# The first steps of a chunked-attention and SoLU-FFN kernel listed anew

## The chip, the cores and the metric

The kernel runs on one core of a Trainium2 chip. The metric is the device time of one execution in microseconds (us). Three runs of the kernel before gave a median of 476.33 us, from 475.26 to 476.84.

## The reference, cut to what matters

Attention in chunks of 64 tokens for 8 batches and 8 heads, then one feed-forward layer on all 4608 tokens. The weights arrive as 8-byte floats, q, k, v as 4-byte ones.

```
q, k, v: (8, 8, 576, 64); chunks of 64
scores = (q_c @ k_c.T) / 8; scores -= max; attn = exp(scores)
attn /= sum(attn) + 1e-9; x = (attn @ v_c) as (4608, 512)
h = x @ w_in                       # (4608, 1024)
sm = softmax(h); solu = h * sm
ln = (solu - mean) / sqrt(var + 1e-6) * g_ln
out = ln @ w_out                   # (4608, 512)
```

## The kernel before

The 4608 tokens are 36 tiles of 128. A tile i goes through transposes of q and k (N), scores (S), a softmax in two parts (A, B), a transpose of the attention (T), values (V), the first product with w_in (M), the SoLU in two parts (X, Y), its variance (R), the turn of z (Z or z) and the second product with w_out in three thirds (F). Products with weights are exact to more bits than one pass gives: each weight and each operand is a high and a low part, and three products are added (24 matmuls of 128x512). Tiles 0 and 1 (`FM = 2`) use the weights whole, in 16 passes, straight from the buffer `w_a`.

The weights are 8 units of 1 MB raw: 0 to 3 are w_in (128 rows each), 4 to 7 are w_out. A unit m is loaded (P), clamped and scaled (c: a clamp on VectorE or GpSimd, then an activation on ScalarE), put together from its two words (C: a shift and a 16-bit addition on VectorE), rounded to its high part (t, ScalarE), and its low part is found for each half (D, the difference, on VectorE or GpSimd). Tile 0's product takes unit m as soon as C:m is done (it is begun in four pieces, one per unit, the four words `M:0`); tile 2's product, the first with three products, needs t and D of units 0 to 3.

Everything before tile 5's product is a list of such steps in one string, `START`. A word is a step; where a step has several parts (a generator), each further mention of the same word runs its next part: `N:1:0` first puts the transposes on TensorE, the second time the copy out of PSUM. `keep_in_program_order` holds every engine's instructions in the order of the list, so each engine takes its own in turn and waits at the first whose data is missing. SyncE (SP) issues nearly all loads, in the list's order too: n is q and k of a tile as they lie in memory (256 KB each), v the values (three loads for a tile below 6 that doesn't straddle two batches), P a unit, q:8 eight of the 32 loads of batch 2's q and k in turned form. W:x is a filler: two matmuls of the identity whose result nobody reads. Two PSUM banks `po` are shared by N, T, z, G and F; during `START` the scores have one bank (`sx`) and the values one (`sy`), and the first products one pair (`ph`), so S:i+1 waits for A:i, V:i+1 for the read of V:i, and M:i+1 for the last read of M:i's result by Y:i (VectorE).

From tile 5 on a loop runs at a fixed order. Its first TensorE steps are M:5, S:8, V:6, S:9, V:7 and then the second product of tile 2. V:6 and V:7 read an attention that U:6 and U:7 turned on VectorE and that SP and GpSimd then move by DMA (`attn_t<-a_b`), and tile 2's operand comes by the DMAs of Z:3 (`z_t<-z_b`).

The tuples ahead of the pools say which engine does a part: `NV_DVE` copies of N on VectorE (else ScalarE), `CL_DVE` clamps on VectorE (else GpSimd), `TV_DVE` copies of T, `NORM_POOL` normalisations (B) on GpSimd (else VectorE), `SUB_POOL` the low parts (D) on GpSimd, `MEAN_POOL` the shift by the mean (Y's second part) on GpSimd (else ScalarE).

Of the kernel before, what the change touches and what calls it, by code (L numbers as in the profile page):

```python
# [12 lines left out]
AF = mybir.ActivationFunctionType  # L13
# [3 lines left out]


START = """
W:41 W:42 n:0 n:1 N:0:1 N:0:0 N:0:0 N:0:1 N:1:0 n:2 S:0 N:2:1 N:1:0 A:0 A:0 P0 P1 P:2 N:1:1 B:0  # L20
P:1 c:0 c:2 N:1:1 W:43 c:0 N:2:0 S:1 W:44 W:45 W:46 N:2:1 N:2:0 n:3 c:2 C:0 A:1 A:1 C:0 B:0 c:1
B:1 S:2 T:0 N:3:0 T:0 W:47 g W:4 c:1 N:3:0 A:2 v:0 C:2 N:3:1 P:3 G P:4 t:0 V:0 N:3:1 n:4 C:1 B:1
G V:0 A:2 S:3 C:1 C:2 T:1 B:2 B:2 c:3 c:3 M:0 t:2 M:0 A:3 C:3 T:1 M:0 v:1 A:3 C:3 c:4 B:3 M:0
N:4:1 X:0 t:1 N:4:0 c:4 n:5 N:4:1 T:2 v:2 B:3 N:4:0 n:6 X:0 V:1 C:4 v:3 P:5 P:6 D:1:0 T:2 Y:0
S:4 T:3 C:4 N:5:0 V:1 A:4 t:3 A:4 P:7 T:3 D:1:1 M:1 t:4 N:5:1 D:3:1 B:4 D:2:1 N:5:0 D:0:1 D:2:0
D:0:0 Y:0 N:5:1 V:2 N:6:1 D:3:0 v:4 D:4:0 N:6:0 c:5 B:4 D:4:1 V:2 S:5 X:1 n:7 N:6:1 X:1 V:2 Y:1
z:0:1 N:6:0 V:3 z:0:1 c:5 R:0 A:5 z:0:0 C:5 A:5 z:0:0 V:3 C:5 M:2 z:0:1 T:4 c:6 B:5 z:0:0 V:3
Q:2 S:6 t:5 c:6 N:7:0 T:4 X:2 C:6 V:4 q:8 v:5 N:7:0 B:5 n:8 D:5:1 c:7 D:5:0 T:5 X:2 Y:2 C:6 T:5
F c:7 Y:2 t:6 C:7 N:7:1 C:7 N:7:1 D:6:1 D:6:0 M:3 F t:7 D:7:0 A:6 V:4 N:8:0 V:4 D:7:1 R:2 q:8
Y:1 N:8:0 V:5 S:7 X:3 Z:2 X:3 N:8:1 Y:3 A:7 N:8:1 A:6 q:8 q:8 F z:1:0 z:1:0 R:1 A:7 B:6 v:6  # L30
z:1:0 M:4 V:5 B:7 B:6 Y:3 U:6 o:0 B:7 Z:3 z:1:1 U:7 z:1:1 v:7 X:4 o:0 X:4 F z:1:1 Y:4 R:3 F K:9
F o:1 Y:4 o:1 V:5 R:4
"""


# [23 lines left out]
def chunk_attention_then_solu_ffn(  # L59
# [35 lines left out]
    MS = nc.gpsimd
    ORD = 5
# [28 lines left out]
    g_sb = const.tile([P, NFC], F32, name="g_sb")  # L125
    g_row = const.tile([NFC, P], F32, name="g_row")
# [10 lines left out]
    HALF = FF // 2  # L137
    raw_words = 2 if w_in.dtype != F32 else 1
# [28 lines left out]
    def unit_scale(x):  # L167
# [71 lines left out]
    QT, KT, V, QS, KS = {}, {}, {}, {}, {}  # L239
# [98 lines left out]
    def turn_natural(i, x):  # L338
# [25 lines left out]
    def attn(i, part):  # L364
        return (sx, sy)[i % 2 if order.on else part][:, :, part]
# [46 lines left out]
    def softmax_b(i):  # L412
# [15 lines left out]
    def attn_transpose(i):  # L428
# [148 lines left out]
    def solu_b(i):  # L577
# [162 lines left out]
    def load_first():  # L740
        load_pair(0)
        sync.dma_start(*early[0])
# [57 lines left out]
    def product():  # L800
# [150 lines left out]
```

## Time and profile before

| | |
|---|---|
| median of 3 runs | 476.33 us |
| the profiled execution | 477.21 us |
| its span | 475.3 us |
| TensorE busy, share of the span | 97% |
| VectorE, ScalarE, GpSimd | 78%, 53%, 34% |

The profile is of one execution: the time outside its span is 1.91 us. Engines are PE (TensorE), PEld (its weight loads), DVE (VectorE), ACT (ScalarE), POOL (GpSimd), SP (SyncE); SPq is the issue of a DMA on SP. A busy TensorE can be one at half its clock; the granted clock stands in the windows as PEclk, 1.00 being full.

### The profile page before, as it was taken

The numbers are of one execution on the slowest core, as the hardware profiler recorded it, in microseconds if no ns is written. First come the engines' busy times: TensorE is split into PE (matmuls) and PEld (weight loads), VectorE is DVE, ScalarE is ACT, GpSimd is POOL, SyncE is SP. The second block draws the span as 40 slices with busy tenths as digits, with TensorE's granted clock in tenths as the row PEclk, the third lists the DMA queues.
The fourth block names the chain that finished last, engine by engine and source line by source line (L and its number), as shares of the span: only waits on it lengthen the run. The fifth ranks groups of instructions, "written<-read, shape, count | busy, mean of one in ns | idle before, by whom it ended". The sixth has DMA issues, their size and how long they took to land.

```text
span 475.3 us, 10986 instructions
## 1 busy us (share of the span) xinstructions
PE 461.9 (97%) x4193; PEld 378.3 (80%) x4193; DVE 368.8 (78%) x511; ACT 249.9 (53%) x402; POOL 160.2 (34%) x305
## 2 busy tenths in 40 slices
PE   6699999999999999999999999999999999999996
PEld 5555888888888888888888888888888888888886
DVE  2799988798888787878788878797979797945430
ACT  2565985546464645454545555555555555554551
POOL 0338556350505050505050505032515141413300
PEclk9799999999999999999999999999999999999999
DMA  9999877878787877697348596948644435333211
GB/s 225 302 248 325 135 134 154 197 181 161 173 164 174 157 179 143 154 168 172 84 125 167 140 188 147 181 123 182 152 111 110 113 85 140 97 103 103 75 44 46
DMA packets 192996, 72.05 MB, mean 152 GB/s; under 512 B 177128, under 2 KB 177648, under 8 KB 192560
## 3 DMA queue, kind: packets, MB, share of 16 engines
q1 hardware_dynamic: 186528, 58.63, 55.4%
q0 software_dynamic: 6272, 12.60, 10.1%
q8 instruction: 33, 0.54, 0.5%
q14 instruction: 19, 0.16, 0.1%
q10 hardware_dynamic: 144, 0.13, 0.1%
HBM read 36.70 MB, written 9.44 MB: 97 GB/s over the span
## 4 chain that ended last, share of the span: by engine, by line
PE 94%; DMA 2%; SPq 2%; DVE 1%; issue 0%; DVEq 0%
PE po L50 44%; PE ph L50 42%; PE sx L50 5%; PE sy L50 4%; DMA nat_z<-in_q_dram 2%; SPq L50 2%; DVE w_a L50 0%; DVE z L50 0%; DVE h_nmax L50 0%; DVE qT L50 0%; DVE o_sb L50 0%; DVEq L50 0%
## 5 line engine op out<-in xcount | busy, mean ns | idle before, releaser
L50 PE MATMUL po<-wo_l,z_h 128*128 128x512 f32 x280 | 110.8, 396 | 0.0
L50 ACT ACTIVATE z<-ph,h_nmax 128x1024 f32<-128x1024 f32 x36 | 40.2, 1117 | 131.6 <-DVE h_nmax L50 131.5
L50 PE MATMUL po<-wo_h,z_h 128*128 128x512 f32 x280 | 109.3, 390 | 0.0
L50 PE MATMUL po<-wo_h,z_l 128*128 128x512 f32 x280 | 109.2, 390 | 0.0
L50 PE MATMUL ph<-wi_l,x_h 128*128 128x512 f32 x272 | 106.1, 390 | 0.0
L50 PE MATMUL ph<-wi_h,x_h 128*128 128x512 f32 x272 | 105.8, 389 | 0.0
L50 POOL TENSOR_TENSOR u<-ssq,eps 128x1 f32<-128x1 f32 x36 | 6.8, 189 | 225.6 <-ACT sq L50 225.6
L50 POOL DMA_DIRECT2D z_t<-z_b x136 | 67.7, 505 | 16.6 <-DVE z_b L50 10.5
L50 PE MATMUL ph<-wi_h,x_l 128*128 128x512 f32 x272 | 72.7, 389 | 0.0
L50 DVE TENSOR_REDUCE h_nmax<-ph 128x1 f32<-128x1024 f32 x36 | 44.0, 1221 | 34.8 <-PE ph L50 34.8
L50 PEld LDWEIGHTS po<-wo_l,z_h 128*128 128x128 f32 x280 | 52.5, 188 | 11.4
L50 PEld LDWEIGHTS po<-wo_h,z_l 128*128 128x128 f32 x280 | 52.6, 188 | 11.0
L50 PEld LDWEIGHTS po<-wo_h,z_h 128*128 128x128 f32 x280 | 52.6, 188 | 10.4
L50 PEld LDWEIGHTS ph<-wi_l,x_h 128*128 128x128 f32 x272 | 51.1, 188 | 10.7 <-issue 0.2
L50 PEld LDWEIGHTS ph<-wi_h,x_l 128*128 128x128 f32 x272 | 51.0, 188 | 10.6
L50 PEld LDWEIGHTS ph<-wi_h,x_h 128*128 128x128 f32 x272 | 51.1, 188 | 10.5
L50 DVE TENSOR_TENSOR z_l<-z_t,z_h 128x1024 fp32r<-128x1024 f32 (+1 forms) x35 | 40.7, 1164 | 21.0 <-ACT z_h L50 21.0
L50 DVE SCALAR_TENSOR_TENSOR z<-ph,z 128x1024 f32<-128x1024 f32 x36 | 44.0, 1224 | 13.8 <-ACT z L50 13.7
L50 ACT ACTIVATE z<-z,z_sum 128x1024 f32<-128x1024 f32 x34 | 39.2, 1153 | 21.4 <-DVE z L50 20.3
L50 DVE STREAM_TRANSPOSE z_b<-z 128x1024 f32<-128x1024 f32 x33 | 39.9, 1209 | 6.6 <-ACT z L50 3.1
L50 ACT ACTIVATE o_sb<-po,r 128x512 f32<-128x512 f32 (+1 forms) x36 | 24.3, 675 | 28.5 <-POOL r L50 20.8
L50 ACT ACTIVATE sq<-z 128x1024 bf16<-128x1024 f32 x36 | 37.6, 1043 | 2.5 <-POOL z L50 2.5
(88 smaller groups left out, 621.8 us busy)
## 6 DMA issues: line engine op xcount, KB each, us to landing
out_dram<-o_sb SPq DMA_DIRECT2D x35, 256.0 KB, 2.5
z_t<-z_b SPq DMA_DIRECT2D x128, 64.0 KB, 2.9
z_t<-z_b POOLq DMA_DIRECT2D x128, 64.0 KB, 2.8
q_st<-in_q_dram SPq DMA_DIRECT2D x96, 72.0 KB, 3.2
k_st<-in_k_dram SPq DMA_DIRECT2D x96, 72.0 KB, 2.9
v_sb<-in_v_dram SPq DMA_DIRECT2D x27, 256.0 KB, 4.3
w_raw<-in_moe_w_out_dram SPq DMA_DIRECT2D x4, 1024.0 KB, 7.2
attn_t<-a_b POOLq DMA_DIRECT2D x60, 64.0 KB, 3.6
```

Of the source, the lines that this page charges most:

```text
L50: ins = make(*args, **kwargs)
```

## The change

The list `START` is replaced by another with the same steps: the eight fillers, every transpose, product and load occur in both. v of tile 0 is loaded third (after q and k of tile 0), units 0 and 1 ahead of q and k of tile 2, unit 2 behind them as two loads of half its columns, unit 3 right behind that and ahead of tile 3. The parts are dealt to the engines anew. g goes by ScalarE's DMA queue. Units 4 and 5 (`GM_ACT`) are multiplied by g on ScalarE in place and then copied to the high part by a second ScalarE instruction, so that the low part is a plain difference.

```diff
 START = """
-W:41 W:42 n:0 n:1 N:0:1 N:0:0 N:0:0 N:0:1 N:1:0 n:2 S:0 N:2:1 N:1:0 A:0 A:0 P0 P1 P:2 N:1:1 B:0
-P:1 c:0 c:2 N:1:1 W:43 c:0 N:2:0 S:1 W:44 W:45 W:46 N:2:1 N:2:0 n:3 c:2 C:0 A:1 A:1 C:0 B:0 c:1
-B:1 S:2 T:0 N:3:0 T:0 W:47 g W:4 c:1 N:3:0 A:2 v:0 C:2 N:3:1 P:3 G P:4 t:0 V:0 N:3:1 n:4 C:1 B:1
-G V:0 A:2 S:3 C:1 C:2 T:1 B:2 B:2 c:3 c:3 M:0 t:2 M:0 A:3 C:3 T:1 M:0 v:1 A:3 C:3 c:4 B:3 M:0
-N:4:1 X:0 t:1 N:4:0 c:4 n:5 N:4:1 T:2 v:2 B:3 N:4:0 n:6 X:0 V:1 C:4 v:3 P:5 P:6 D:1:0 T:2 Y:0
-S:4 T:3 C:4 N:5:0 V:1 A:4 t:3 A:4 P:7 T:3 D:1:1 M:1 t:4 N:5:1 D:3:1 B:4 D:2:1 N:5:0 D:0:1 D:2:0
...
+n:0 W:41 W:45 W:43 N:0:1 v:0 N:0:0 n:1 W:42 P0 P1 c:0 P:1 N:0:1 n:2 N:0:0 P:2 W:44 S:0 N:1:0
+A:0 N:1:0 A:0 N:1:1 W:4 N:1:1 P:3 B:0 c:0 B:0 S:1 A:1 A:1 T:0 T:0 n:3 N:2:0 c:1 v:1 v:3
+c:1 N:2:1 N:2:1 n:4 W:47 N:2:0 W:46 v:2 C:0 C:0 V:0 c:2 C:1 C:1 n:5 S:2 P:5 V:0 B:1 B:1
+T:1 g A:2 c:2 P:4 t:1 C:2 c:3 c:3 T:1 C:2 M:0 M:0 N:3:0 t:2 M:0 C:3 A:2 N:3:1 C:3
+t:3 P:6 M:0 B:2 B:2 D:3:1 D:3:0 N:3:0 N:3:1 T:2 X:0 D:1:0 V:1 V:1 S:3 D:2:0 T:2 N:4:1 X:0 N:4:0
+V:2 A:3 N:4:1 N:4:0 t:0 S:4 Y:0 P:7 n:6 V:2 Y:0 R:0 A:4 M:1 D:1:1 D:0:0 A:3 B:3 A:4 V:2
+v:4 c:5 B:4 N:5:1 B:4 B:3 D:2:1 c:4 T:3 N:5:1 T:3 N:5:0 X:1 T:4 X:1 n:7 D:0:1 v:6 V:3 T:4
+N:5:0 S:5 Y:1 G A:5 c:4 C:4 z:0:1 c:5 c:6 G M:2 c:6 z:0:1 C:4 C:6 z:0:1 V:3 C:6 t:4
+D:4:1 X:2 N:6:1 N:6:1 z:0:0 N:6:0 n:8 D:4:0 c:7 V:3 X:2 N:6:0 V:4 Y:2 t:6 D:6:1 C:5 A:5 C:5 S:6
+B:5 B:5 Y:2 V:4 Z:2 z:0:0 z:0:0 N:7:0 v:5 t:5 D:6:0 D:5:1 D:5:0 N:7:0 R:2 M:3 X:3 T:5 F F
+T:5 X:3 V:4 Y:3 Y:1 c:7 C:7 N:7:1 N:7:1 Q:2 A:6 C:7 M:4 t:7 D:7:0 A:6 z:1:0 z:1:0 Y:3 D:7:1
+q:8 B:6 B:6 z:1:0 F q:8 X:4 S:7 A:7 q:8 R:1 v:7 V:5 o:0 z:1:1 z:1:1 U:6 q:8 z:1:1 F
+N:8:0 F Z:3 A:7 N:8:0 N:8:1 X:4 B:7 Y:4 R:3 N:8:1 B:7 V:5 Y:4 V:5 R:4 U:7 o:0 K:9 F
+o:1 o:1
...
-    NV_DVE = ((0, 1), (1, 0), (2, 1), (4, 0), (6, 1), (9, 1),)
-    MEAN_POOL = (3, 4,)
-    CL_DVE = (0, 3, 4,)
-    TV_DVE = (3,)
-    SUB_POOL = ((0, 0), (0, 1), (1, 0), (1, 1), (2, 0), (2, 1), (3, 0), (3, 1), (7, 0), (7, 1),)
-    NORM_POOL = (0, 1, 2, 3, 4, 5, 6, 7,)
+    NV_DVE = ((0, 1), (1, 1), (5, 0), (6, 0), (7, 1), (8, 1), (9, 1))
+    MEAN_POOL = (1, 3)
+    CL_DVE = (1, 3)
+    TV_DVE = ()
+    GM_ACT = (4, 5)
+    SUB_POOL = ((0, 1), (1, 0), (1, 1), (2, 0), (3, 0), (4, 0), (4, 1), (5, 1), (6, 1))
+    NORM_POOL = (0, 4, 5, 6)
...
-    XV_DVE = ()
+    HALF_IN = (2,)
+    XV_DVE = (1, 2)
...
                 g = g_sb[:, 2 * m + y:2 * m + y + 1]
-                act.activation(top[:, y], a[:, y], AF.Copy, scale=g)
+                act.activation(
+                    a[:, y] if x in GM_ACT else top[:, y], a[:, y], AF.Copy, scale=g
+                )
+            if x in GM_ACT:
+                act.copy(top, a)
...
-        sync.dma_start(g_row, g_ln.rearrange("(a p) -> a p", p=P))
+        nc.scalar.dma_start(g_row, g_ln.rearrange("(a p) -> a p", p=P))
```

## Rows read from the trace of the kernel before

**Rows 1.** The page: busy times, then the chain that ended last
```profile
PE 461.9 (97%) x4193; PEld 378.3 (80%) x4193; DVE 368.8 (78%) x511; ACT 249.9 (53%) x402; POOL 160.2 (34%) x305
...
PE 94%; DMA 2%; SPq 2%; DVE 1%; issue 0%; DVEq 0%
```

**Rows 2.** Waits of TensorE from 0 to 40 us: total, times, longest
```profile
PE sx L50 <- DVE e L50: 2.9, 1, 2.9
...
PE po L50 <- DMA nat_z<-in_q_dram: 1.1, 1, 1.1
PE ph L50 <- DVE z L50: 0.9, 1, 0.9
```

**Rows 3.** Timeline of TensorE: start, length, what, idle before it
```profile
18.27 0.66 PE L50 MATMUL po<-ident,e 128*128 128x128 f32 x4
20.04 1.09 PE L50 MATMUL po<-ident,nat_z 128*128 128x128 f32 x4 [1.12 <-DMA nat_z<-in_q_dram]
...
26.23 7.15 PE L50 MATMUL ph<-w_a,x_f 128*128 128x512 f32 x16
...
38.27 7.10 PE L50 MATMUL ph<-w_a,x_f 128*128 128x512 f32 x16 [0.95 <-DVE z L50]
```

**Rows 4.** Windows: stretch, length, busy by engine, PEclk, DMA share, GB/s
```profile
6.00:7.00 1.00, 1.00 (x6) 0.87 (x5) 0.55 (x1) 0.00 (x0) 0.00 (x0) 1.00 1.40 218
11.00:12.00 1.00, 0.68 (x7) 0.49 (x6) 0.62 (x1) 0.83 (x2) 0.00 (x0) 1.00 1.08 434
23.00:24.00 1.00, 1.00 (x12) 0.65 (x13) 0.07 (x1) 0.22 (x1) 0.00 (x0) 0.50 1.04 418
...
45.00:60.00 15.00, 15.00 (x225) 12.12 (x224) 14.53 (x20) 12.88 (x23) 9.37 (x9) 1.00 0.85 181
```

**Rows 5.** Timeline of SP's DMA issues
```profile
9.71 5.12 SPq L50 DMA_DIRECT2D nat_z<-in_k_dram  x1
14.87 2.76 SPq L50 DMA_DIRECT2D g_row<-in_moe_g_ln_dram  x1
...
20.08 0.60 SPq L50 DMA_DIRECT2D w_raw<-in_moe_w_in_dram  x1
...
60.70 6.90 SPq L50 DMA_DIRECT2D q_st<-in_q_dram  x8
67.72 9.83 SPq L50 DMA_DIRECT2D k_st<-in_k_dram  x16
...
78.71 5.39 SPq L50 DMA_DIRECT2D z_t<-z_b  x8
84.27 2.42 SPq L50 DMA_DIRECT2D attn_t<-a_b  x4
```

**Rows 6.** Timeline: the first clamps of units 0 and 1
```profile
13.59 0.69 DVE L50 TENSOR_SCALAR w_a<-w_raw 128x1024 f32<-128x1024 f32 x1 [1.27 <-DMA w_raw<-in_moe_w_in_dram]
...
18.88 1.42 POOL L50 TENSOR_SCALAR w_a<-w_raw 128x1024 f32<-128x1024 f32 x1 [0.71 <-DMA w_raw<-in_moe_w_in_dram]
```

**Rows 7.** Groups of the tile w_a, 13 to 66 us: shortest/median/longest ns
```profile
L50 ACT ACTIVATE w_a<-w_a x8: 1057/1057/1079, 14.3 to 59.3; 128x1024 f32<-128x1024 f32 x8
L50 DVE TENSOR_SCALAR w_a<-w_a x8: 667/684/1830, 15.4 to 61.4; 128x1024 uint32<-128x1024 uint32 x8
L50 DVE SCALAR_TENSOR_TENSOR w_a<-w_raw,w_a x8: 1326/1382/2248, 17.4 to 62.1; 128x1024 uint16<-128x1024 uint32 x8
L50 POOL TENSOR_TENSOR wi_l<-w_a,wi_h x8: 1265/1277/2301, 33.9 to 45.5; 128x512 fp32r<-128x512 f32 x8
...
L50 DVE SCALAR_TENSOR_TENSOR wo_l<-w_a,g_sb,wo_h x6: 726/736/1758, 43.3 to 64.1; 128x512 fp32r<-128x512 f32 x6
```

**Rows 8.** DMA issues at 86.4 us: KB each, us from issue to landing
```profile
attn_t<-a_b SPq DMA_DIRECT2D x1, 64.0 KB, 2.2
```

**Rows 9.** Timeline of TensorE where the attention moved by DMA is first read
```profile
89.69 0.75 PE L50 MATMUL sx<-attn_t,v_sb 64*64 64x64 f32 x29
```

**Rows 10.** The chain that ended last, in order of time, at M:2
```profile
49.88 5.67 PE ph L50 x24
```

More of the change, by code (lines that the diff above doesn't have):

```diff
@@ L19 @@
 START = """
-W:41 W:42 n:0 n:1 N:0:1 N:0:0 N:0:0 N:0:1 N:1:0 n:2 S:0 N:2:1 N:1:0 A:0 A:0 P0 P1 P:2 N:1:1 B:0
-P:1 c:0 c:2 N:1:1 W:43 c:0 N:2:0 S:1 W:44 W:45 W:46 N:2:1 N:2:0 n:3 c:2 C:0 A:1 A:1 C:0 B:0 c:1
-B:1 S:2 T:0 N:3:0 T:0 W:47 g W:4 c:1 N:3:0 A:2 v:0 C:2 N:3:1 P:3 G P:4 t:0 V:0 N:3:1 n:4 C:1 B:1
-G V:0 A:2 S:3 C:1 C:2 T:1 B:2 B:2 c:3 c:3 M:0 t:2 M:0 A:3 C:3 T:1 M:0 v:1 A:3 C:3 c:4 B:3 M:0
-N:4:1 X:0 t:1 N:4:0 c:4 n:5 N:4:1 T:2 v:2 B:3 N:4:0 n:6 X:0 V:1 C:4 v:3 P:5 P:6 D:1:0 T:2 Y:0
-S:4 T:3 C:4 N:5:0 V:1 A:4 t:3 A:4 P:7 T:3 D:1:1 M:1 t:4 N:5:1 D:3:1 B:4 D:2:1 N:5:0 D:0:1 D:2:0
[L26 to L32, printed above, removed]
+n:0 W:41 W:45 W:43 N:0:1 v:0 N:0:0 n:1 W:42 P0 P1 c:0 P:1 N:0:1 n:2 N:0:0 P:2 W:44 S:0 N:1:0
[12 more added lines that the diff above has]
+o:1 o:1
 """
@@ L161, in load_pair @@
         else:
-            sync.dma_start(dst, src)
+            cut = HALF * raw_words if x in HALF_IN else 2 * HALF * raw_words
+            if x >= NCC:
+                sync.dma_start(dst, src)
+            else:
+                for n in range(0, 2 * HALF * raw_words, cut):
+                    sync.dma_start(dst[:, n:n + cut], src[:, n:n + cut])
         raws[x] = raw
@@ L221, in unit_rest @@
             low = wo_l[:, 2 * m + y, :]
-            g = g_sb[:, 2 * m + y:2 * m + y + 1]
+            if x not in GM_ACT:
+                g = g_sb[:, 2 * m + y:2 * m + y + 1]
         of, part = a[:, y], top[:, y].bitcast(F32)
```

## The prediction

> **What bounds the kernel now.** I read busy times and the chain first [rows 1]: TensorE is busy for 97% of the span and makes 94% of the chain that ended last, so an edit counts only if TensorE begins its work earlier or is stopped later. Then where it stands still: its waits are all ahead of 40 us [rows 2], the last one 0.9 us in front of tile 1's product, which starts at 38.27 [rows 3]. From there it has one instruction behind the other to the end. Third, its clock [rows 4]: PEclk is 0.50 in the window at 23 us (full would be 2.4 GHz, this is 1.2), after the engine had done nothing from 18.93 (18.27 + 0.66) to 20.04 and, before that, for the 2.9 us of the longest wait; a set of four transposes then takes 1.09 us [rows 3]. By 26.23 it is back: tile 0's 16 passes take 7.15 us, tile 1's 7.10. Fourth, why it waits: for scores behind VectorE (2.9 us), and for q of tile 3 (1.1) [rows 2]. Loads all go through SP, which is held at 9.71 for 5.12 us by k of tile 3 and then for 2.76 us by the tiny g, so that unit 3 is issued only at 20.08 [rows 5].
>
> The steps are the same before and after, the eight fillers too. So two questions: how much earlier, for the same work done, TensorE has its unbroken run, and whether the new deal among the engines breaks that run later.
>
> **The loads.** q, k and v move at 218 GB/s, weights at 434 [rows 4]: 256 KB (0.262 MB) take 1.2 us, a unit (1.05 MB) 2.4 us. v of tile 0 now lies ahead of the units (+1.2), q and k of tile 2 behind units 0 and 1 (-2.4). Unit 0 was there at 13.59 [rows 6]: now 13.59 - 2.4 + 1.2 = 12.4. The third unit in the queue was there at 18.88 [rows 6]; the second now at 18.88 - 2.4 - 2.4 + 1.2 = 15.3, the third (unit 2, with tile 2 ahead again) at 20.1, unit 3 right behind at 22.5. Tile 2's q, by tile 3's of before (20.04, three units and three tiles ahead of it [rows 3]), comes at 20.04 - 2.4 - 2.4 + 1.2 = 16.4, its k at 17.6; tile 3's at 20.04 + 2.4 + 1.2 = 23.6 and 24.8. Unit 2's two halves cost SP one more issue (0.6 at most [rows 5]) and gain nothing, as its clamp reads both. g leaves SP: that frees 2.76 us, which only the loads behind tile 3 see; on ScalarE it costs between nothing and the same 2.76 us. I take 0.5, hidden, as no step of TensorE waits for ScalarE there by less than that.
>
> **Up to tile 0's product.** Unit 0's clamp is now on GpSimd (1.1, at most 1.42 [rows 6]) and tile 0's normalisation behind it, another 1.1: T:0 at 14.6 in place of 18.27. TensorE then waits for tile 2 until 16.4, so its clock will fall as before. From 16.4 it has N:2, two fillers, V:0, S:2, T:1; before, from 20.04 to 26.23, it had the same kinds of steps and G, at the low clock for most of it: 6.2 us [rows 3]. So M:0 begins at 22.6, 3.6 earlier. But N:3's two sets, done before M:0 in the old order, now stand between its pieces (1.2 us): it ends at 22.6 + 7.15 + 1.2 = 31.0, in place of 33.4. Are the units there? Unit 2: 20.1, clamp 1.1, ScalarE 1.06, shift 0.7, addition 1.35 [rows 7], with some 2 us behind other steps: 26.3, wanted at 26.8. Unit 3: 22.5, the same chain with its clamp behind unit 2's shift on VectorE: 28.2, wanted at 29.2. Both just make it.
>
> **Tile 1's product.** After M:0 VectorE takes the maximum, ScalarE the exponential and VectorE the product before `ph` is free: 38.27 - 33.4 = 4.9 us before [rows 3]. The new list puts tile 1's x and tile 3's softmax between them on VectorE, where a copy and unit 4's shift stood. That shift was one of the slow ones (up to 1.83 us where 0.68 is usual [rows 7]). I keep 4.9: M:1 at 35.9, 2.4 earlier. Less work lies ahead of it, though: T:3, half of N:5 and G come later than they did, V:2 earlier, 0.6 + 0.6 + 0.2 - 0.6 = 0.8. The net gain is 1.6 us.
>
> **The engines' new parts.** VectorE gets four normalisations, three low parts of w_in, tile 1's x and one more copy of N (nine parts), and gives up two parts of w_out, a copy of T and a clamp (four). None of the nine stands in the trace there; by the nearest row each costs between 0.7 and 1.76 us [rows 7], and I take 0.7: five more parts, 3.5 us. From 45 to 60 us VectorE was busy for 14.53 of 15 us [rows 4], so that is not free; before, it ran late behind a TensorE that had other work. GpSimd loses three low parts (1.28 each [rows 7]) and four normalisations, and gains a clamp and about one part of w_out. ScalarE gets two copies of a unit (GM_ACT, bounded by its own activation of that size, 1.06 each) and a little more; at 12.88 of 15 us it can carry that. A VectorE that is late shows at the start of M:2, M:3 and M:4, which wait for its last read of `ph`. Bounds for what this takes back: nothing, and the whole 1.6. I take 0.4, the gap I find when I put VectorE's steps around M:2 and M:3 behind one another (some 0.1 to 0.25 at each).
>
> **A rule of the skill.** Two parts of VectorE and GpSimd at once: an addition of 1.33 us takes up to 2.25, a low part of 0.73 up to 1.76, while GpSimd's differences run [rows 7]. The Trainium skill (SBUF — State Buffer, section Who interferes with whom) says that a VectorE instruction with two SBUF inputs and a GpSimd one that reads SBUF exclude each other for a whole instruction. The trace's longest times agree. By that rule seven of the parts that move to VectorE are of the kind that can be held. That speaks against the change; it is the second rival.
>
> **Sum.** -1.6 + 0.4 = -1.2 us on the profiled 477.21, of which 475.3 is span: 476.0. That execution is 0.9 above the median of the runs, so I put it on the median: 476.33 - 1.2 = 475.1. Own range, with the low clock ending 1 us earlier or later: 474.2 to 476.0.
>
> **Rivals.**
> First, more is gained. VectorE keeps up (0.4 not lost), the low clock ends sooner, so that M:0 begins 0.7 earlier (units 2 and 3, each with under a microsecond in hand, let no more through), and M:0 to M:1 shrinks by the 1.15 us (1.83 - 0.68) that the slow shift had cost: -1.2 - 0.4 - 0.7 - 1.15 = -3.45, 472.9. For it: that shift stands between no product and its result any more. Against it: TensorE still has over 3 us of gaps between 12 and 17.6, and more such gaps made the clock fall before.
> Second, VectorE becomes the bound. Seven moved parts held by half a GpSimd difference each (0.64) are 4.5 us more on an engine with half a microsecond free in 15; against that GpSimd is less busy. They are spread over M:1 to M:4, each with 4 to 5 us of other TensorE steps as cover; between nothing and 4.5 I let 1.9 through: -1.6 + 1.9 = +0.3, the gain is gone, 476.6.
> Third, the other side: SP is late for tiles 6 and 7. n:8 now stands ahead of all 32 loads of batch 2 and must wait until N:6:0 has read the buffer: M:1 ends at 35.9 + 7.1 = 43.0, eight short steps are 4.4, M:2 5.5 (5.67 with its first wait [rows 10]), three sets 1.7, so 54.6. Behind it on SP queue v of tile 5, the 32 loads, v of tile 7, then Z:3's and U:7's transfers, which V:6 reads. n:8 and the two v move in 4.8 us, of which SP, a load ahead, sees 3.7. The loads take 23.6 if 16 of them go as the eight at 60.70 (6.90 twice) and 16 as those at 67.72 (9.83 [rows 5]); Z:3 then gets the queue at 81.9, where it had it at 78.71. U:7's last transfer, begun at 86.1 (84.27 + 3/4 of 2.42), landed 2.2 later, at 88.3 [rows 5, 8], and V:6 read at 89.69 [rows 9]: 1.4 to spare. So TensorE would wait 3.2 + 1.2 - 1.4 = 3.0 us and the sum is +1.8: 478.1. It decides once the loads take over 20.6 us; at 0.61 each, the rate of the 16, they take 19.7 and nothing is late. For it: the eight at 60.70 stood right behind the same two steps. Against it: the queue will have been empty while SP waits for N:6:0.
> That the units don't come earlier at all, because SP is held at tile 2's k as it was at tile 3's, is in the second's price: a hold until about 12 us still leaves unit 2's data unbroken.
>
> **Numbers.** Some 0.3% (1.43 us) is what a measurement of this kernel tells from no change: 474.9 to 477.8. Forecast 0.40, first rival 0.25, second 0.15, third 0.20. Faster: 0.17 of the forecast (its lower end is below 474.9) and the first, 0.42. Same: 0.23 of the forecast, 0.11 of the second, 0.04 of the third, 0.38. Slower: the rest, 0.20. The range reaches from a little beyond the first rival's gain to the third's full price: 472.6 to 478.2.
>
> **What would show it.** Right: unit 3's load issued by 12 us in place of 20.08; T:0 near 14.6; M:0 starting near 22.6 and ending near 31, M:1 near 35.9; Z:3's transfers issued no later than 79. Wrong: PEclk at 0.50 beyond 24 us, a wait of TensorE in front of M:2, M:3 or M:4 on VectorE of over 0.5 us, or one on `attn_t` near 88 us.

## The result and the profile after

The changed kernel takes 478.82 us (median of 13 runs, 478.09 to 481.28); the kernel before, on the same chips, 475.97 (13 runs, 475.26 to 477.74). The ratio is 1.0054, 95% interval 1.0040 to 1.0069: slower, by some 2.6 us, where 1.2 us less were forecast. The profiled execution took 478.68 us, with a span of 476.9.

The page of the changed kernel, busy times and then the chain that ended last:

```profile
PE 463.0 (97%) x4193; PEld 379.1 (79%) x4193; DVE 371.3 (78%) x516; ACT 251.0 (53%) x403; POOL 153.7 (32%) x300
...
PE 85%; SPq 6%; DVE 4%; ACT 2%; DMA 2%; issue 1%; DVEq 0%; ACTq 0%
```

Beside [rows 1], TensorE's share of the chain falls from 94% to 85%; the share of SP's queue rises from 2% to 6%, VectorE's from 1% to 4%, and ScalarE has 2%. The timeline of TensorE (start, length, what, idle before it) shows where:

```profile
15.02 0.80 PE L51 MATMUL po<-ident,e 128*128 128x128 f32 x4 [2.56 <-POOL e L51]
...
22.76 3.60 PE L51 MATMUL ph<-w_a,x_f 128*128 128x512 f32 x8
...
29.07 1.88 PE L51 MATMUL ph<-w_a,x_f 128*128 128x512 f32 x4
...
33.75 1.06 PE L51 MATMUL po<-ident,nat 128*128 128x128 f32 x8 [1.26 <-DMA nat<-in_k_dram]
...
36.48 7.13 PE L51 MATMUL ph<-w_a,x_f 128*128 128x512 f32 x16
...
57.47 0.63 PE L51 MATMUL po<-ident,nat 128*128 128x128 f32 x4 [0.90 <-DMA nat<-in_q_dram]
...
91.41 0.63 PE L51 MATMUL sx<-attn_t,v_sb 64*64 64x64 f32 x27 [0.82 <-DMA attn_t<-a_b]
...
98.53 0.39 PE L51 MATMUL ph<-wi_l,x_h 128*128 128x512 f32 x1
```

The front is as forecast: M:0 from 22.76 to 30.95 us and M:1 at 36.48, where [rows 3] have 26.23 and 38.27. Then come three waits on transfers that the kernel before didn't have in its first profile (in a second one its N:4 waits 0.15 us): N:4 for k of tile 4, N:7 for q of tile 7, V:6 for `attn_t` (it read at once in [rows 9]). The last row is M:6. From there to the end of the span it is 378.4 us here (476.9 - 98.53) and within 0.1 us of that in every profile of the table further down, so M:6's start says all.

To see what comes before M:6, take the windows (stretch, length, busy time of PE, PEld, DVE, ACT, POOL, granted clock, DMA share, GB/s). The changed kernel:

```profile
30.00:36.00 6.00, 4.59 (x124) 3.49 (x125) 5.96 (x7) 4.11 (x8) 4.30 (x3) 1.00 0.79 168
36.00:46.00 10.00, 9.76 (x70) 5.22 (x66) 7.34 (x14) 6.18 (x11) 5.14 (x6) 1.00 1.03 366
46.00:66.00 20.00, 18.72 (x211) 15.56 (x212) 19.61 (x26) 17.57 (x29) 14.50 (x13) 1.00 0.83 180
66.00:86.00 20.00, 19.95 (x156) 16.05 (x155) 17.62 (x28) 12.98 (x25) 8.46 (x15) 1.00 0.84 151
86.00:98.53 12.53, 11.71 (x170) 9.64 (x169) 10.57 (x15) 6.28 (x10) 3.51 (x9) 1.00 0.83 171
```

The kernel before, in a second profile of it taken for the study (477.24 us):

```profile
30.00:36.00 6.00, 5.52 (x48) 2.76 (x50) 5.26 (x8) 4.77 (x9) 2.99 (x3) 1.00 0.73 147
36.00:46.00 10.00, 9.40 (x89) 5.08 (x83) 9.70 (x11) 5.33 (x9) 8.56 (x7) 1.00 1.10 276
46.00:97.07 51.07, 51.07 (x568) 42.25 (x565) 43.35 (x62) 36.87 (x64) 28.11 (x37) 1.00 0.84 176
```

Length less busy PE is idle TensorE; busy PE from 30 us to M:6 is the work that was left at 30 us. Before: 1.08 us idle, 66.0 us of work, and no idle time at all from 46 us on. After: 3.80 us idle, 64.7 us of work. So the changed kernel had done 1.3 us more by 30 us and then lost 2.7 us. VectorE was busy for 19.61 of the 20 us from 46 to 66; but in the kernel before it was so for 19.41, and TensorE never stopped there. That VectorE is full doesn't show by itself that TensorE waits for it.

SP's issues in the changed kernel (start, length, what, count), against [rows 5]:

```profile
17.32 10.28 SPq L51 DMA_DIRECT2D v_sb<-in_v_dram  x6
27.72 1.27 SPq L51 DMA_DIRECT2D nat<-in_q_dram  x2
...
37.97 8.48 SPq L51 DMA_DIRECT2D nat<-in_k_dram  x1
46.51 5.61 SPq L51 DMA_DIRECT2D v_sb<-in_v_dram  x4
52.21 0.55 SPq L51 DMA_DIRECT2D nat<-in_q_dram  x1
...
60.48 9.57 SPq L51 DMA_DIRECT2D q_st<-in_q_dram  x16
70.17 4.43 SPq L51 DMA_DIRECT2D k_st<-in_k_dram  x8
...
75.19 6.03 SPq L51 DMA_DIRECT2D k_st<-in_k_dram  x8
81.32 5.04 SPq L51 DMA_DIRECT2D z_t<-z_b  x8
86.53 2.43 SPq L51 DMA_DIRECT2D attn_t<-a_b  x4
```

Six loads of v (tiles 1 and 3) hold SP for 10.28 us, and only then can it issue q and k of tile 4, at 27.72. k of tile 6 and v of tile 4 hold it from 37.97 to 52.12, behind the four units of w_out; q of tile 7 goes at 52.21. Z:3's transfers go at 81.32, where they went at 78.71 [rows 5], with 16 + 8 + 8 loads ahead of them.

VectorE's instructions that matter, in the changed kernel:

```profile
30.18 1.76 DVE L51 TENSOR_TENSOR wi_l<-w_a,wi_h 128x512 fp32r<-128x512 f32 x1
31.87 1.21 DVE L51 TENSOR_REDUCE h_nmax<-ph 128x1 f32<-128x1024 f32 x1
...
34.92 1.22 DVE L51 SCALAR_TENSOR_TENSOR z<-ph,z 128x1024 f32<-128x1024 f32 x1
...
79.48 1.23 DVE L51 STREAM_TRANSPOSE z_b<-z 128x1024 f32<-128x1024 f32 x1
...
84.98 0.70 DVE L51 STREAM_TRANSPOSE a_b<-e 128x512 f32<-128x512 f32 x1
```

D:3:1, one of the parts that moved to VectorE, takes 1.76 us and stands ahead of tile 0's maximum, which starts 0.9 us behind M:0's end. Y:0, which frees `ph` for M:1, ends at 36.14, only 0.34 us ahead of M:1's start: had N:4 not waited its 1.26 us, VectorE would have held M:1 for most of that. In the same way Z:3 (79.48) ends at 80.7, 0.6 us ahead of the issue of its transfers: SP's loads and VectorE reach that point together.

### The profile page after: what moved, and what is told of

Its sections match the earlier page's. It is cut to its first block, busy times and chain, and to the rows that moved or that the text cites. A ratio compares the mean times of both kernels' runs of the same rounds, so it can differ in the third digit from the quotient of the medians.

```text
span 476.9 us, 10982 instructions
## 1 busy us (share of the span) xinstructions
PE 463.0 (97%) x4193; PEld 379.1 (79%) x4193; DVE 371.3 (78%) x516; ACT 251.0 (53%) x403; POOL 153.7 (32%) x300
## 4 chain that ended last, share of the span: by engine, by line
PE 85%; SPq 6%; DVE 4%; ACT 2%; DMA 2%; issue 1%; DVEq 0%; ACTq 0%
PE po L51 40%; PE ph L51 37%; SPq L51 6%; PE sx L51 4%; PE sy L51 3%; DVE w_a L51 1%; ACT z L51 1%; DMA v_sb<-in_v_dram 1%; DMA attn_t<-a_b 1%; DVE z L51 1%; DVE wo_l L51 0%; DVE h_nmax L51 0%; ACT sq L51 0%; DVE z_l L51 0%; DVE z_b L51 0%
## 5 line engine op out<-in xcount | busy, mean ns | idle before, releaser
L51 ACT CAST z_h<-z_t 128x1024 fp32r<-128x1024 f32 (+1 forms) x35 | 34.7, 992 | 6.5 <-PE po L51 4.7
```

The costliest lines, as they stand in the source:

```text
L51: ins = make(*args, **kwargs)
```

## The experiments

Two theories. **Loads**: the new list issues some transfers late, and TensorE waits for them. **VectorE**: the parts that moved to VectorE, and its order, are the bound, and the waits on transfers only stand in front of VectorE's. Each ratio is to the kernel before on the same chip.

**The list alone.** The new `START` with the old deal, and units 4 and 5 made the old way.

```
-    NV_DVE = ((0, 1), (1, 1), (5, 0), (6, 0), (7, 1), (8, 1), (9, 1))
+    NV_DVE = ((0, 1), (1, 0), (2, 1), (4, 0), (6, 1), (9, 1),)
...
-    NORM_POOL = (0, 4, 5, 6)
+    NORM_POOL = (0, 1, 2, 3, 4, 5, 6, 7,)
```

> The new list with the old deal of parts among the engines (g still by ScalarE's queue, unit 2 in halves). Two theories for the 2.6 us by which the changed kernel is slower. VectorE theory: the parts dealt to VectorE are held by GpSimd and it reaches the maximum and the last read of each first product late; then the list alone is no slower than before: within 0.7 us of it, and the low part D:3:1 no longer stands in front of tile 0's maximum. Loads theory: SP's order is what costs (tile 7's q and k behind four units of w_out, tile 8's ahead of all 32 loads of batch 2); then the list alone is as slow as the whole change, 2 to 3.5 us over before, and V:6 waits for the moved attention by 0.5 us or more.

507.36 us, 1.0648 (1.0625 to 1.0670). TensorE's waits (who waits for whom, us in total, times, longest):

```profile
PE po L51 <- POOL e L51: 7.2, 3, 4.7
```

**The deal alone.** The old `START` with the new tuples; g on SP, unit 2 whole.

> The old list with the new deal of parts (units 4 and 5 multiplied by g in place on ScalarE too). VectorE theory: slower than before by 1.5 us or more, with TensorE waiting ahead of M:2 or M:3. Loads theory: within 1 us of before, since SP's order is the old one.

487.76 us, 1.0249 (1.0223 to 1.0275). Its waits:

```profile
PE po L50 <- DVE kT L50: 4.7, 2, 3.2
PE ph L50 <- DVE x_f L50: 3.5, 1, 3.5
```

Both expectations were far off. Neither half can stand without the other: every engine takes its steps in order, so a list fits the deal for which it was made. The longest waits are for a part that the deal puts on that engine (normalisations on GpSimd here, a copy of N and tile 1's x on VectorE there). But the two runs don't decide between the theories: the deal alone, 12 us slower, changes parts of all three engines at once.

**The loads of batch 2 earlier**, so that SP is free before Z:3.

```
-... N:6:0 n:8 D:4:0 ... C:5 A:5 C:5 S:6
+... N:6:0 D:4:0 ... C:5 A:5 C:5 Q:2 q:8 q:8 n:8 S:6
-... v:5 t:5 ... Q:2 A:6 ... \ q:8 B:6 B:6 z:1:0 F q:8 X:4 S:7 A:7 q:8 R:1 ... U:6 q:8
+... v:5 q:8 t:5 ... A:6 ... \ B:6 B:6 z:1:0 F q:8 X:4 S:7 A:7 R:1 ... U:6
```

> The changed kernel, but the first 16 loads of batch 2 are listed ahead of tile 8's q and k, and the others right behind v of tile 5, so that SP need not wait for N:6:0 before them. Loads theory: Z:3's transfers get SP's queue at 79 or earlier in place of 81.3, the 0.8 us wait of V:6 for the moved attention goes, and the time falls by 1 to 1.6 us below the changed kernel's. VectorE theory: the wait may go, but M:3 and what follows stay as late as they are, and the time is the changed kernel's within 0.5 us.

478.74 us, 1.0053 (1.0034 to 1.0073): no gain. Its TensorE and then its SP:

```profile
70.65 0.50 PE L51 MATMUL ph<-wi_l,x_h 128*128 128x512 f32 x1 [0.65 <-DVE z L51]
...
93.72 0.63 PE L51 MATMUL sx<-attn_t,v_sb 64*64 64x64 f32 x27 [0.61 <-DMA attn_t<-a_b]
```

```profile
70.70 8.91 SPq L51 DMA_DIRECT2D k_st<-in_k_dram  x16
...
83.25 5.40 SPq L51 DMA_DIRECT2D z_t<-z_b  x8
```

After one more load (0.50 at 79.66) SP now stands still from 80.16 to 83.25, waiting for Z:3 on VectorE, and V:6 still waits (0.61 in place of 0.82). N:7's wait is gone in this profile, and M:4 waits 0.65 us for VectorE's last read of `ph` instead. The profiled execution was the slowest of its six, 480.96 us: behind N:4's wait of 1.47 us the granted clock fell to between 0.50 and 0.66 from 36 to 40 us, and M:1 took 7.84 us in place of 7.13. Its waits can be read, its total can't be compared.

**Units 6 and 7 later**, behind n:6 and v:4.

```
-t:3 P:6 M:0 ... Y:0 P:7 n:6 ... v:4 c:5
+t:3 M:0 ... Y:0 n:6 P:6 ... v:4 P:7 c:5
```

> The changed kernel, but units 6 and 7 are listed behind tile 6's q and k and v of tile 4, so that these and tile 7's don't queue behind 4 MB of weights. Loads theory: the 0.9 us wait of N:7:0 goes, M:3 starts at about 57.2 in place of 57.95, 0.5 to 1 us are won. VectorE theory: M:3 is then held by VectorE's last read of M:2's result, which ended at 57.1, so 0.7 at most comes back.

480.57 us, 1.0080 (1.0055 to 1.0106): no gain, and the interval overlaps that of the changed kernel. N:7's wait for q is gone, but ScalarE stands still for 3.17 us until the later unit is clamped (52.42) and copies k of tile 6 only at 56.65; N:7 waits 1.76 us for that bank, at 57.28.

**v of tile 3 behind n:4 and v:2**, so that q and k of tile 4 are issued sooner.

```
-N:2:0 c:1 v:1 v:3 c:1 N:2:1 N:2:1 n:4 W:47 N:2:0 W:46 v:2
+N:2:0 c:1 v:1 c:1 N:2:1 N:2:1 n:4 W:47 N:2:0 W:46 v:2 v:3
```

> The changed kernel with the load of v of tile 3 (v:3) listed behind n:4 and v:2 and not ahead of them, so that SP issues q and k of tile 4 some 3 to 4 us sooner. In the changed kernel N:4 waits 1.26 us for k of tile 4, ahead of M:1. Loads theory (the changed kernel's loss is in waits for transfers that the new list issues late): the wait goes and the lead stays, 478.8 - 1.2 = 477.6 us. VectorE theory (each such wait only covers one for VectorE right behind it): M:1 then waits for Y:0, which ended 36.14 us in the changed kernel against M:1's start at 36.48, so at most 0.3 us is gained (478.5) and the trace shows a wait of some 0.9 us of M:1 or of V:2 or S:4 on VectorE.

478.78 us, 1.0041 (1.0025 to 1.0057). TensorE:

```profile
32.58 0.69 PE L51 MATMUL sy<-attn_t,v_sb 64*64 64x64 f32 x32 [0.22 <-DVE x_f L51]
...
34.19 0.69 PE L51 MATMUL sx<-kT,qT 64*64 64x64 f32 x32 [0.91 <-ACT qT L51]
...
67.11 0.50 PE L51 MATMUL ph<-wi_l,x_h 128*128 128x512 f32 x1 [0.65 <-DVE z L51]
```

The wait for k is gone, and 1.29 us of idle time remain between 30 and 36 us where 1.41 were: V:2 waits for VectorE (its read of V:1's result), S:4 for ScalarE. The gain of 0.0013 (some 0.6 us) lies within the intervals; the profile is of the fastest of the six runs (477.44 us), and what it has over the changed kernel's is mostly less work left at 30 us.

**D:3:1 and D:5:0 on GpSimd**, alone and with v of tile 3 later.

```
-    SUB_POOL = (..., (4, 0), (4, 1), (5, 1), (6, 1))
+    SUB_POOL = (..., (4, 0), (4, 1), (5, 1), (6, 1), (3, 1), (5, 0))
```

> The changed kernel with D:3:1 and D:5:0 back on GpSimd and nothing else. v:3 moved alone gave 1.0041 of the time before, both together 1.0030, the changed kernel 1.0054. If the waits cover each other: X:0 comes 1 us sooner, N:4 still waits for k of tile 4, M:1 starts no sooner, and the time is within 0.3 us of the changed kernel's. If they add: 0.5 us faster (1.0043).

> The same, and the two subtractions D:3:1 and D:5:0 go back from VectorE to GpSimd (in the changed kernel they took 1.76 and 1.78 us there, in front of the maxima of tiles 0 and 3). VectorE theory: X:0 starts at M:0's end (1.0 us sooner), Y:0 ends about 35.1, the gain behind N:4 comes free: 478.8 - 1.2 = 477.6 us or a little less. Loads theory: the same as v:3 moved alone. If GpSimd with two more parts is late instead, M:2 or M:4 waits for wi_l or the store's products for wo_l, and the time is above 479.

Of the two, only D:3:1 had moved with the change: D:5:0 was VectorE's in the kernel before too, with the multiplication by g in the same instruction, and D:5's two parts took 1.40 us together there (57.35 in the first profile). Alone 478.74 us, 1.0037 (1.0022 to 1.0051); with v of tile 3 later 478.20, 1.0030 (1.0017 to 1.0043). Together the idle time between 30 and 36 us falls to 0.63; alone it stays at 1.33. The intervals of the four kernels of this square (1.0054, 1.0041, 1.0037, 1.0030) overlap from one to the next; the order of their waits is the better evidence. The profile with both has one stop of 1.15 us inside M:2 that waits for nothing that is shown, so its M:6 says little.

**Z:3 and U:7 earlier on VectorE**, on top of the earlier loads.

```
-B:6 B:6 z:1:0 F q:8 X:4 ... F Z:3 A:7 ... X:4 B:7 Y:4 R:3 N:8:1 B:7 V:5 Y:4 V:5 R:4 U:7 o:0
+q:8 B:6 B:6 z:1:0 Z:3 F X:4 ... F A:7 ... X:4 B:7 B:7 U:7 Y:4 R:3 N:8:1 V:5 Y:4 V:5 R:4 o:0
```

> The changed kernel with the loads of the third batch listed earlier (as in the run with these loads moved alone, 478.74 us, where SP was idle for 3 us ahead of z_t and attn_t came no sooner), and besides Z:3 on VectorE 3.9 us sooner and B:7's normalisation and U:7 ahead of Y:4 (about 2.4 us sooner). Theory that VectorE's order sets attn_t: z_t is issued by SP about 77 to 78 us, attn_t about 83, V:6's wait of 0.82 us goes, 478.0 us. Theory that SP sets it: no gain over the loads moved alone. Theory that Z:3 ahead of X:4 only moves the price: M:5 waits for Y:4 instead, 478.8.

479.07 us, 1.0055 (1.0035 to 1.0075). SP issues z_t at 77.80 and `attn_t` at 84.73, V:6 no longer waits, and nothing is gained: ahead of N:8 stands a new wait, as long.

```profile
80.95 0.66 PE L51 MATMUL po<-ident,nat 128*128 128x128 f32 x4 [0.79 <-DVE z_l L51]
```

The part z_l that N:8 waits for had slipped behind U:6 on VectorE. The third theory held, at another place than it had named.

**All of it together**, then with U:6 behind that z_l as well.

```
-V:5 o:0 z:1:1 z:1:1 U:6 z:1:1 F
+V:5 o:0 z:1:1 z:1:1 z:1:1 U:6 F
```

> All of it together: v:3 later, D:3:1 and D:5:0 on GpSimd, the third batch's loads earlier, Z:3 and U:7 earlier. If the loss of the changed kernel is the sum of the waits found (N:4 1.26, N:7 0.90 or M:4's 0.65 behind it, V:6 0.82 us), it goes almost whole: 478.8 - 2.7 = 476.1 us, level with the kernel before. If VectorE's work is the bound of the whole stretch up to 90 us wherever it stands, not over 1 us is gained: 477.8 or more.

> The run of all three with U:6 behind the last part of z:1:1 on VectorE. There V:6 no longer waited, but N:8 waited 0.79 us for the bank that this part (z_l) reads, 0.7 us behind U:6. Theory that each wait is one place in VectorE's order: N:8's wait falls to about 0.1 us and no other comes, 478.3 - 0.7 = 477.6 us, some 0.15% over the kernel before. Theory that VectorE is full there: U:7 comes 0.6 us later and M:5 or V:6 waits instead, 478.3.

478.27 us, 1.0027 (1.0012 to 1.0042), and with U:6 moved 476.84 us, 1.0017 (1.0002 to 1.0032). Idle time behind 30 us falls from 3.8 to 2.67 and 2.17 us. Of all these lists only the last has an interval clear of the changed kernel's (1.0040 to 1.0069). TensorE's waits of 0.3 us in the last one still pass from queue to engine to engine:

```profile
56.91 0.63 PE L51 MATMUL po<-ident,nat 128*128 128x128 f32 x4 [0.34 <-DMA nat<-in_q_dram]
...
65.21 0.51 PE L51 MATMUL po<-wo_l,z_h 128*128 128x512 f32 x1 [0.34 <-POOL wo_l L51]
...
79.71 0.66 PE L51 MATMUL po<-ident,nat 128*128 128x128 f32 x4 [0.20 <-DVE z_l L51]
```

**Tile 0's normalisation ahead of unit 0's clamp** on GpSimd, V:0 ahead of N:2, on top of the last.

```
-P0 P1 c:0 P:1 ... B:0 c:0 B:0 S:1 ... T:0 T:0 n:3 N:2:0 ... C:0 C:0 V:0 ... P:5 V:0 B:1
+P0 P1 P:1 ... B:0 B:0 c:0 c:0 S:1 ... T:0 T:0 n:3 V:0 V:0 N:2:0 ... C:0 C:0 ... P:5 B:1
```

> The same, and in front B:0's normalisation ahead of unit 0's clamp on GpSimd (in the changed kernel the clamp waits there for unit 0's landing until 12.85 us, and the normalisation, ready at 12.64, ran at 13.92, so that T:0 waited 2.56 us), and V:0 ahead of N:2. If T:0 sets the front: T:0 about 1 us sooner and M:0 too, 476.6 us. If the front is set by units 2 and 3 (landing and conversion, M:0's last part at 29.07 us right behind unit 3's shift and add): M:0 starts sooner and ends at the same time, no gain, 477.6.

478.63 us, 1.0052 (1.0035 to 1.0069): 1.8 us worse. T:0 came at 14.20, but unit 0's activation now stood ahead of the copy of T:0 on ScalarE, V:0 waited 2.51 us for it, and N:2 behind it.

**The small parts, undone**: g on SP's queue again; unit 2 in one load.

```
-        nc.scalar.dma_start(g_row, g_ln.rearrange("(a p) -> a p", p=P))
+        sync.dma_start(g_row, g_ln.rearrange("(a p) -> a p", p=P))
```
```
-    HALF_IN = (2,)
+    HALF_IN = ()
```

> The changed kernel with g on SP's queue again, at its place in the new list (ahead of units 4 to 7 and of q and k of tiles 6 and 7). In the kernel before g held SP 2.8 to 3.1 us, and there its move to ScalarE's queue changed nothing (1.0000), since the next load was held as long instead. If that holds here: within 0.3 us of the changed kernel. If SP's order is what limits N:7 (0.90 us for q of tile 7): up to 2.8 us later, 479.5 to 481.

> The changed kernel with unit 2 of the weights loaded in one transfer, not in halves. M:0's end is set by unit 3's landing and conversion (M:0's last part at 29.07 us, right behind unit 3's add at 28.73), so no change by over 0.3 us. If the halves let unit 2 or what follows it land sooner, M:0's third part (26.82) comes later and the time rises by up to 1 us.

479.50 us, 1.0058 (1.0038 to 1.0078), and 479.27 us, 1.0056 (1.0041 to 1.0071): neither can be told from the changed kernel's 1.0054.

**The changed kernel and the kernel before once more**, one profiled run each.

> The changed kernel, unchanged, for a second profile. If its loss is what the first profile shows: 3.5 to 4 us of TensorE idle from 30 us to M:6's start, with the waits of N:4 for k of tile 4 (1.26 us), of N:7 for q of tile 7 (0.90) and of V:6 for attn_t (0.82) within 0.3 us again, and 64 to 65.5 us of work left at 30 us. If the waits move about from run to run, none of the three is a place to mend and the loss is the front's spread.

> The kernel before, unchanged, for a second profile: its first one took 477.21 us, 1.2 us above the median of its runs, with 1.28 us of TensorE idle from 30 us to M:6's start (96.96 us) and 65.7 us of work left at 30 us; the changed kernel has 3.79 us and 64.7 us. Theory that the changed kernel's loss is idle time behind 30 us: about 1 us idle again, whatever the front does. If instead the kernel before usually reaches 30 us with less work left than in its first profile, that is where the medians' difference beyond the profiles' 1.5 us lies: M:6 starts near 95.8, work left near 64.5.

479.01 and 477.24 us. The changed kernel's second profile has 3.67 us idle behind 30 us and 65.1 us of work left (3.80 and 64.7 in the first), but not the same waits:

```profile
33.84 1.07 PE L51 MATMUL po<-ident,nat 128*128 128x128 f32 x8 [1.53 <-DMA nat<-in_k_dram]
...
68.56 0.50 PE L51 MATMUL ph<-wi_l,x_h 128*128 128x512 f32 x1 [0.62 <-DVE z L51]
...
91.61 0.63 PE L51 MATMUL sx<-attn_t,v_sb 64*64 64x64 f32 x27 [0.60 <-DMA attn_t<-a_b]
```

q of tile 7 was there in time, and M:4 waited for VectorE instead: the same exchange as with the loads moved. The kernel before repeats too (1.28 and 1.08 us idle, 65.7 and 66.0 us of work).

**The kernel before with one part of the change, and with one of the findings**: g by ScalarE's queue; the shift of unit 4 behind Y:0; both.

```
-N:4:0 n:6 X:0 V:1 C:4 v:3 P:5 P:6 D:1:0 T:2 Y:0
+N:4:0 n:6 X:0 V:1 v:3 P:5 P:6 D:1:0 T:2 Y:0 C:4
```

> The kernel before with one part of the change alone: g by ScalarE's queue. In the kernel before, SP was held 2.76 us by g at 14.87 us, ahead of q and k of tile 3. By the prediction's working these come some 2 us sooner, N:3's wait of 1.12 us goes, and M:0 follows by 0.5 to 1 us: 475.6. If the transfers share the same bandwidth and SP's wait only shows it, no change: 476.3 within 0.3.

> The kernel before with the shift of unit 4 (C:4's first part, 1.83 us at 35.15 beside a GpSimd subtraction, in front of Y:0) listed behind Y:0. In the kernel before M:1 waited 0.95 and 0.60 us in the two profiles for Y:0 (36.91 to 38.12 us; ScalarE had its exponential ready at 35.9), and TensorE had no idle time from there to M:6. VectorE theory: Y:0 ends about 37.1, M:1's wait goes, and since nothing else waits behind it, the whole 0.6 to 0.95 us stays: 475.3 to 475.7 us (0.998). Theory that the next wait takes it: unit 4's conversion is 1.2 us later, M:1's end or N:5 or N:6 waits, no change.

> The same with g by ScalarE's queue. In the run with g alone M:0 started 0.6 us sooner and M:1 at the same 38.36 us, held 0.95 us by Y:0. If Y:0's place was all that held it: as much as without g or up to 0.3 us better, 475.0 to 475.6 us. If M:0's end (33.4 us, set by units 3's conversion on VectorE) is the floor: the same as without g.

With g moved: 476.95 us, 1.0000 (0.9982 to 1.0018). M:0 starts 0.7 us sooner (25.64) than in the second profile, M:1 at the same 38.36, held 0.95 us by VectorE: M:0's last piece waits 0.53 us for unit 3's conversion on VectorE, and M:0 ends at 33.46, as in the second profile (33.47). With the shift behind Y:0: 475.86 us, 0.9988 (0.9979 to 0.9998). Both: 475.95 us, 0.9990 (0.9977 to 1.0002). So the one exchange on VectorE gave some 0.6 us, the best of the study and the only kernel whose interval ends below 1, if barely. VectorE in the kernel before (second profile), and then with the exchange:

```profile
35.33 1.74 DVE L50 TENSOR_SCALAR w_a<-w_a 128x1024 uint32<-128x1024 uint32 x1
36.99 1.21 DVE L50 SCALAR_TENSOR_TENSOR z<-ph,z 128x1024 f32<-128x1024 f32 x1
...
38.14 2.27 DVE L50 SCALAR_TENSOR_TENSOR w_a<-w_raw,w_a 128x1024 uint16<-128x1024 uint32 x1
```

```profile
35.49 1.23 DVE L50 SCALAR_TENSOR_TENSOR z<-ph,z 128x1024 f32<-128x1024 f32 x1 [0.68 <-ACT z L50]
...
36.64 0.69 DVE L50 TENSOR_SCALAR w_a<-w_a 128x1024 uint32<-128x1024 uint32 x1
37.36 1.31 DVE L50 SCALAR_TENSOR_TENSOR w_a<-w_raw,w_a 128x1024 uint16<-128x1024 uint32 x1
```

The shift and the addition behind it, 4.01 us in the one place, take 2.00 in the other, and Y:0 ends at 36.7 in place of 38.2. Of these 1.5 us the exchange made some 1.0: from M:0's end to M:1's start it is 3.92 us in place of 4.89. The other 0.5 came from the front, where this run's granted clock was higher (0.86 for 0.70 from 20 to 30 us).

The account of the profiles, but for the list alone and the deal alone (idle and work in us from 30 us to M:6's start, worked out from windows as above; work includes any stretch at a lower clock):

| kernel | M:6 at | idle | work left | ratio |
|---|---|---|---|---|
| before, first and second | 96.96, 97.07 | 1.28, 1.08 | 65.7, 66.0 | 1 |
| changed, first and second | 98.53, 98.78 | 3.80, 3.67 | 64.7, 65.1 | 1.0054 |
| loads of batch 2 earlier | 100.84 | 3.52 | 67.3 | 1.0053 |
| units 6 and 7 later | 101.48 | 5.16 | 66.3 | 1.0080 |
| v of tile 3 later | 97.22 | 3.29 | 63.9 | 1.0041 |
| D:3:1, D:5:0 on GpSimd | 99.16 | 3.52 | 65.6 | 1.0037 |
| these, and v of tile 3 later | 98.37 | 3.89 | 64.5 | 1.0030 |
| loads earlier, Z:3 and U:7 earlier | 98.90 | 3.45 | 65.5 | 1.0055 |
| v, D, loads, Z:3 and U:7 together | 97.46 | 2.67 | 64.8 | 1.0027 |
| and U:6 later | 97.68 | 2.17 | 65.5 | 1.0017 |
| and tile 0's normalisation first | 98.42 | 2.11 | 66.3 | 1.0052 |
| changed, g on SP again | 99.39 | 4.08 | 65.3 | 1.0058 |
| changed, unit 2 in one load | 98.78 | 3.67 | 65.1 | 1.0056 |
| before, g by ScalarE's queue | 97.07 | 1.81 | 65.3 | 1.0000 |
| before, shift behind Y:0 | 95.35 | 0.78 | 64.6 | 0.9988 |
| before, both | 95.22 | 0.93 | 64.3 | 0.9990 |

## Why the prediction was wrong

**The front came as forecast.** T:0 was forecast at 14.6 and came at 15.02, M:0 22.6 and 22.76, its end 31.0 and 30.95, M:1 35.9 and 36.48 (first profile; the second is within 0.4 us of it). From M:0's end to M:1 it was 5.5 us where 4.9 was kept. Units 2 and 3 made it with less in hand than was said: their additions end at 26.76 and 28.73, 0.06 and 0.34 us ahead of their pieces of M:0 (0.5 and 1.0 forecast). One sign failed on the way: unit 3's load was issued at 15.57, not by 12, since SP was held for 3.54 us by k of tile 2 and for 3.50 by the first half of unit 2, and its clamp began at 24.79, not 22.5. The gain in work done was 1.6 us by the sum, and 0.6 to 1.3 at 30 us between one profile and another.

**The step that failed is "I take 0.4"**, for what is taken back behind the front. It measured 2.4 to 2.7 us (3.67 and 3.80 us idle less 1.28 and 1.08), more than its upper bound, the whole 1.6. The step looked at VectorE around M:2 and M:3 alone. Three things were not in it:

- SP's queue ahead of tile 4. Moving v of tiles 1 and 3 ahead of n:4 was not priced; SP is at them for 10.28 us, and N:4 waits 1.26 and 1.53 us. With v of tile 3 behind, q of tile 4 is issued at 24.58 in place of 27.72 and this wait is gone.
- A second wait right behind each wait. VectorE's Y:0 ends 0.34 us ahead of M:1's start although N:4 has waited; M:4 waits 0.62 us for VectorE when N:7 doesn't wait for its load. Taking away the wait for k left 1.29 of 1.41 us, taking away V:6's wait put 0.79 at N:8. This is why each repair alone gave 0.8 us or less, and three and four together 1.3 and 1.8 (ratios 1.0027 and 1.0017 against 1.0054).
- V:6, off by its size and half by its cause. The third rival had Z:3's transfers at 81.9 (81.32 measured) and a wait of V:6 on `attn_t`, but priced it at 3.0 us (0.6 to 0.8 measured) and put it down to SP alone. The 32 loads took 20.0 us (9.57 + 4.43 + 6.03), less than the 20.6 from which it was to decide; SP was 0.6 us behind VectorE's Z:3 at that point, and with SP free (the loads of batch 2 earlier), Z:3's end at 83.22 set the issue at 83.25. The new list has Z:3 2.0 us and U:7 6.4 us later on VectorE than the old one (77.44 and 78.60 in the first profile), which no term priced.

**The rivals.** The first (more gained) didn't happen: tile 0's maximum stood behind a part held by GpSimd again, D:3:1 in place of the shift. Its term of 1.15 us for the shift was near what the kernel before could gain: the exchange there took 1.0 us off that stretch. The second had a mechanism that occurs, but for seven parts held by 0.64 us each; the trace has two of the seven held, D:3:1 (1.76 us) and tile 1's normalisation (1.03, beside a clamp on GpSimd), some 1.4 us over what they take alone, and the other five at 0.64 to 0.69. Its 1.9 us and the third's 3.0 were given as cases apart, each to be had without the other; here parts of both came, with N:4's wait, which was in neither, and together they exceeded the gain. PEclk was full from 23 us on. Of the signs named for being wrong, the wait on `attn_t` and the one of over 0.5 us on VectorE ahead of M:4 (in the second profile) were seen; Z:3's transfers came after 79, against the last sign for being right.

**What g was worth.** The forecast freed 2.76 us on SP with g's move. In the kernel before with g moved, SP is held by the next load as long:

```profile
9.44 5.28 SPq L50 DMA_DIRECT2D nat_z<-in_k_dram  x1
14.77 5.14 SPq L50 DMA_DIRECT2D v_sb<-in_v_dram  x3
```

In the kernel before, g and these three took 2.76 + 2.36 us together in the first profile and 3.10 + 2.80 in the second. In the changed kernel with g back on SP, g took 0.41 us. So the hold is not g's own. That it belongs to the data ahead in the queue fits these three numbers, but no run varied that data alone.

**What stays open.** The medians lie 2.6 us apart by the ratio, the profiles 1.5 to 1.8. The two profiles of the kernel before took 477.2 us, 0.3 to 1.2 over its medians in the six comparisons (475.97 to 476.96), and there is none of a shorter run. Both have a mean granted clock of 0.70 to 0.71 from 20 to 30 us; the two kernels with the shift behind Y:0, with the same list up to there but for g, had 0.86 and 1.00 in that stretch and 64.6 and 64.3 us of work left at 30 us. The kernel before with g moved had 0.83 and 65.3. A kernel before that keeps the clock would be that much further and would leave the changed kernel no lead, which would account for the rest. The mean granted clock of every run, which is on record, speaks for it: of the 87 runs of the kernel before beside the experiments, the 22 at 0.993, the value of both its profiles, have a median of 477.37 us, the 40 at 0.995 to 0.998 one of 476.79, and the 18 at 0.999 or 1.000 one of 476.04, while none of the changed kernel's 13 runs is above 0.998. The 7 at 0.991 and 0.992, with 476.14, don't fit, and no run of the kernel before with the full clock was profiled, so where these gain their time is not shown.

The repairs, too, leave 2.17 us idle where the kernel before has 1.1 to 1.3. Whether the list itself or VectorE's work bounds that remainder was not told apart.

## What to carry to other kernels

In a list where every engine takes its steps in order, a wait in the trace is only the last of several that end close together: before pricing its removal, look up when the other operands and engines of that step were ready, and take the difference to the second latest as the most that can be gained. When a change pulls the front forward and moves work to another engine, count idle time and work left on the bound engine from one fixed moment to the first step behind which all is equal; the two numbers say whether the lead was smaller or was lost later. Then see by the clocks and times of the other runs whether the profiled one was a usual one. List and deal are one thing here: the deal alone was 2.5% slower, the list alone 6.5%.

## What the runs showed of the hardware

VectorE's shift of unit 4 (one input, in place, 128x1024) takes 0.69 us alone and 1.74 when it is issued at 35.33, while GpSimd runs two differences from 34.02 to 36.53 in the second profile of the kernel before:

```profile
34.02 2.51 POOL L50 TENSOR_TENSOR wi_l<-w_a,wi_h 128x512 fp32r<-128x512 f32 x2
37.97 9.36 POOL L50 TENSOR_TENSOR wi_l<-w_a,wi_h 128x512 fp32r<-128x512 f32 x6 [1.44 <-ACT wi_h L50]
```

It ends at 37.07, 0.54 us behind them, which is less than its own 0.69, so the rest was a wait; the addition, issued at 38.14 just behind the start of the next six, takes 2.27. Exchanged with Y:0, they take 0.69 and 1.31: GpSimd's two differences end at 36.01 there, the shift runs from 36.64 in the gap behind them, and the addition, from 37.36, begins 0.08 us ahead of the next six (37.44), of which the first now takes 2.32 us in place of 1.27. Y:0, which reads `ph` in PSUM, runs beside a difference for its first 0.5 us there and takes 1.23, as it does without one (1.21). The Trainium skill (SBUF — State Buffer, section Who interferes with whom) has this: not only instructions with two SBUF inputs but `tensor_scalar` in a mode that uses both ports takes the shared pair, and the one that comes second is blocked for the whole instruction of the first. The trace agrees, with 1.74 against 0.69 for the shift, and with 2.27 against 1.31 for the addition by which of the two engines began first. What a part costs on VectorE thus depends on what GpSimd runs beside it, and one exchange of places was worth some 0.6 us here.
